# Dealing one weight matrix anew over the DMA engines of a decode kernel

## The chip, the cores and the metric

One core of a Trainium2 chip. The time is the device time of one execution in microseconds (us), lower is better. Engines are named as in the profile: PE (TensorE), DVE (VectorE), ACT (ScalarE), POOL (GpSimd), SP (SyncE, which here only issues transfers). The core has sixteen DMA engines.

## The reference

A decode step for four tokens: the input goes through a layer norm, and the sum of three things is returned: the input, an attention block over a cache (A), and a small gated MLP (B).

```python
x = A_x                                     # 4 x 1 x 640
xn = _layernorm(x, axis=-1)
# A: 32 heads of 128, a cache of 4096 positions for each of the 4 tokens
q = (xn @ wq) ...                           # wq 640 x 4096
scores = jnp.einsum('bhqd,bhkd->bhqk', q, k_cache) * Dh ** (-0.5)
p = _softmax(scores, axis=-1)
o = jnp.einsum('bhqk,bhkd->bhqd', p, v_cache)
A = o... @ wo                               # wo 4096 x 640
# B: F = 1728, Fh = 864
z = _gelu(jnp.einsum('bsd,df->bsf', xn, w_in))      # w_in 640 x 1728
z1 = z[..., :Fh]
z2 = _layernorm(z[..., Fh:], axis=-1)
g = jnp.einsum('ts,bsf->btf', w_sp, z2) + b_sp[None, :, None]
B = jnp.einsum('bsf,fd->bsd', z1 * g, w_out)        # w_out 864 x 640
return x + A + B
```

All data is bf16. The two caches are 128 MiB each; the other weights together are about 14 MB.

## The kernel before

**What streams.** K and V come in units: eight heads of one token, 4 MiB, laid on 128 partitions of 64 KiB. There are 16 units of K and 16 of V. The tile `kv` has five slots of 32 KiB per partition, and a unit takes two halves of slots; the dictionary `place` says which. SP issues all these loads from one queue, in the order of `seq`: K0 to K3, then V0, K4, V1, K5 and so on (`load_unit`, line 187). The fourth unit of K of each group of heads and the last unit of V are loaded in two parts (`cuts`). Each load waits until the engines have done with what lay in its slots. A unit is 64 KiB on each partition and eight partitions on each DMA engine.

**A unit of K** (`emit_K`): DVE transposes it in eight instructions (line 419, some 2.3 us each) into the two halves of `kT_t`, and PE multiplies (line 430). After four units come the softmax and the spreading of its weights (`softmax`, `z_fill`). **A unit of V** (`emit_V`): 64 matmuls (line 501), then two DVE instructions. **The end:** the last three parts of A_wo (`load_wo`, line 195), the projections (`o_mul`, line 544), one sum, and the output.

**The start.** SP issues wq (line 126) and w_in (line 129) first. The MLP's second matrix, w_out, lies in the tile `w_words`, which the K transposes use afterwards (`kT_t` is its first part). It is kept as 26 chunks of 640 on 128 partitions; row (partition, chunk) holds one of the 864 rows of w_out, and the places that hold none must be zero. So DVE fills the 8,320 words of each partition with zeros (line 131), and then six pieces are loaded. The table `PC` describes a piece: first and last partition and their step, first chunk, chunks n, the factor i by which its rows are dealt, and the run of consecutive rows:

```python
PC = {"w": (0, 28, 2, 0, 9, 7, 9), "a": (32, 52, 1, 0, 10, 5, 10), "n": (68, 92, 2, 0, 8, 6, 8),
      "l": (92, 95, 1, 0, 26, 2, 13), "b": (1, 12, 2, 0, 26, 3, 26), "s": (60, 68, 1, 0, 26, 2, 26)}
```

`load_piece` (line 136) gives a piece to a queue; the source's outermost dimension is i. Before, SP loads "a" and "b"; GpSimd, with a queue of its own, loads "w", "s", "n" and "l" in that order. Between them SP loads four `marks` (line 144): a few bytes of w_out to 6, 10, 12 and 14 partitions of a scratch tile that nothing reads. A transfer ends by counting up a semaphore; SP's and ACT's transfers use eight of these in turn, and one that takes a semaphore again first waits for the transfer that had it before.

**The MLP.** `xnT` is the normalised input, turned. z is computed by matmuls of 32 columns of PE each (line 328; five chunks c, six matmuls each, into three column groups q and two PSUM tiles `zr_ps`). ACT applies gelu in 16 instructions (`gelu`, lines 339 and 342), which put the columns in their places in `zT`. Then come the statistics (lines 365 to 380), three POOL instructions (381 to 383), a DVE transpose (384), and 52 matmuls with w_out (line 397). Only after the first sixteen of these may the first K unit be transposed into `w_words`; and only when half of it is transposed (four instructions) is the slot free that the third K load needs.

Of the kernel before, what the change touches and what calls it, by code (L numbers as in the profile page):

```python
# [8 lines left out]
ACT = mybir.ActivationFunctionType  # L9
# [3 lines left out]
BF16 = mybir.dt.bfloat16  # L13
# [3 lines left out]
def kernel(  # L17
# [19 lines left out]
    nc = tc.nc  # L37
    P = 128
    B, Sq, D = A_x.shape
    _, H, Sk, Dh = A_k_cache.shape  # L40
    assert Sq == 1 and B == 4 and Dh == P and D % P == 0
    DC = D // P
# [14 lines left out]
    FC = 26  # L57
# [3 lines left out]
    PC = {"w": (0, 28, 2, 0, 9, 7, 9), "a": (32, 52, 1, 0, 10, 5, 10), "n": (68, 92, 2, 0, 8, 6, 8),  # L61
          "l": (92, 95, 1, 0, 26, 2, 13), "b": (1, 12, 2, 0, 26, 3, 26), "s": (60, 68, 1, 0, 26, 2, 26)}
    f_of, f_end = {}, 0
# [4 lines left out]
    NOUT = A_wo.shape[1]  # L68
# [3 lines left out]
    eps = 1e-5  # L72
# [58 lines left out]
    nc.vector.memset(w_words[:, 0:FC * NOUT // 2], 0.0)  # L131
# [7 lines left out]
    load_piece(nc.sync, "a")  # L139
    load_piece(nc.sync, "b")  # L140
    marks = const.tile([14, 288], BF16)
    m0 = 0
    for k, m in ((6, 96), (10, 80), (12, 64), (14, 48)):
        nc.sync.dma_start(out=marks[0:k, m0:m0 + m], in_=B_w_out[0:k, 0:m])
        m0 += m
    sw = load_piece(nc.gpsimd, "w")
    for t in ("s", "n", "l"):
        with tc.issue_after(sw.ins):
            sw = load_piece(nc.gpsimd, t)
# [55 lines left out]
    nc.gpsimd.memset(ones_f[:], 1.0)  # L205
    eps_t = const.tile([P, 1], F32)
    nc.gpsimd.memset(eps_t[:], eps)
# [39 lines left out]
    nc.gpsimd.memset(SelN[:].rearrange("p e x -> p (e x)"), 0.0)  # L247
# [57 lines left out]
    for a in range(2):  # L305
# [13 lines left out]
    z_parts = [(0, 0, w_z[:, :, :, f_of["w"][0]:f_of["w"][1]]), (0, 1, w_z[:, :, :, f_of["a"][0]:f_of["a"][1]]),  # L319
               (0, 2, w_z[:, :, :, f_of["n"][0]:f_of["l"][1]]), (1, 0, w_z[:, :, :, f_of["b"][0]:f_of["b"][1]])]  # L320
    s_src = w_z[:, :, :, f_of["s"][0]:f_of["s"][1]].rearrange("p d a (r i c) -> p d i a r c", i=2, c=PC["s"][4])
    z_parts += [(1, 1 + i, s_src[:, :, i]) for i in range(2)]
    for c in range(DC):
        for bk, q, src in z_parts:
            w = 1
            for m in src.shape[3:]:
                w *= m
            nc.tensor.matmul(zr_ps[bk][32 * q:32 * q + 32, :, 0:w], lhsT=xnT[:, c, :], rhs=src[:, c],  # L328
                             start=(c == 0), stop=(c == DC - 1))
# [4 lines left out]
    def gelu(q, bk, f0, c0, n, x, order=None):  # L334

        z = zr_ps[bk][32 * q:32 * q + 32, :, f0:f0 + len(range(*x)) * n]
        dst = zT[32 * q:32 * q + 32, :, c0:c0 + n, x[0]:x[1]:x[2]]
        if order is None:
            nc.scalar.activation(out=dst, in_=z.rearrange("p a (x c) -> p a c x", c=n), func=ACT.Gelu_apprx_tanh)
        else:  # L340
            for a in range(2):
                nc.scalar.activation(out=dst[:, a].rearrange("p c (i r) -> p c i r", i=order),  # L342
                                     in_=z[:, a].rearrange("p (r i c) -> p c i r", i=order, c=n), func=ACT.Gelu_apprx_tanh)

    gelu(0, 0, 0, 0, 9, (0, 28, 2), 7)
    gelu(1, 0, 0, 0, 10, (0, 20, 1), 5)
    gelu(2, 0, 0, 0, 8, (4, 28, 2), 6)
    f_l = f_of["l"][0] - f_of["n"][0]
    for i in range(2):
        for j in range(3):  # L350
            x = 28 + (3 * i + j) // 2
            gelu(2, 0, f_l + 26 * j + 13 * i, 13 * ((3 * i + j) % 2), 13, (x, x + 1, 1))
    gelu(0, 1, 0, 0, 26, (1, 12, 2), 3)
    gelu(1, 1, 0, 0, 26, (28, 32, 1))
    gelu(2, 1, 0, 0, 26, (0, 4, 1))

    one_bf = const.tile([1, P], BF16)
    nc.gpsimd.memset(one_bf[:], 1.0)
# [284 lines left out]
```

## Time and profile before

| | us |
|---|---|
| median of 3 runs (663.44 to 663.63) | 663.45 |
| the profiled execution's own time | 663.37 |
| its span, first to last instruction | 661.6 |
| DVE busy | 380.1 |
| PE busy | 293.2 |
| wq first packet | 1.7 |
| zero fill of w_out's tile on DVE | 2.53 to 9.52 |
| z matmuls | 25.57 to 28.29 |
| gelu instructions | 29.49 to 32.56 |
| first K transpose | 46.89 |
| third K load issued | 56.03 |
| last transfer of A_wo landed | 658.27 |

On the page, "DMA" is the mean busy share of the sixteen DMA engines in each fortieth of the span, in tenths; q1 is the queue of SP, q0 that of GpSimd, q10 that of ACT, q8 and q14 carry the engines' instructions.

The trace has the start, length, size and queue of each of the 7,112 packets, but not the DMA engine. In a busy stretch a packet starts some 4 ns before or 2 to 3 ns after the end of the one before it on its engine, so the packets can be joined into sixteen streams. From 10 us to the end of A_wo all sixteen then carry the same 368 packets of wq, w_in, K, V and A_wo, each in the same order; they differ in these things alone:

| streams | pieces of w_out on each | bytes of w_out | end of K0, us | instruction fetches on the way | end of the last A_wo packet, us |
|---|---|---|---|---|---|
| 3 | a, b, w | 140,800 | 44.37, 44.54, 44.73 | none | 657.01, 657.17, 657.30 |
| 2 | a, w | 74,240 | 42.22, 42.24 | one and three of 8 KB | 655.67, 657.83 |
| 2 | w | 23,040 | 40.14, 40.54 | two of 16 KB each | 655.99, 656.33 |
| 2 | s | 133,120 | 44.45, 45.14 | one of 8 KB each | 657.78, 657.81 |
| 6 | n | 20,480 | 39.91 to 40.72 | two of 16 KB; the last stream three | 655.69, 655.77, 655.77, 655.88, 656.50, 657.46 |
| 1 | l | 99,840 | 44.03 | none | 656.67 |

(Where two streams are within some 10 ns of each other they can be taken for one another; this happens among the six "n" streams and near 20 us.) The 16 KB fetches come 49.8, 76.2, 113.1, 151.4, 189.9, 229.4, 258.6, 287.4 us after the start, on eight different streams, and then go round the same eight again in the same order; the 17th (634.3) falls to the first and the 18th comes at 656.4.

### The profile page before, as it was taken

The page shows a single profiled execution, that of the slowest core. Times are in us where ns is not written, and L with a number is a line of the kernel's source. Part 1 is how long each engine was busy: PE and PEld are TensorE (multiplying, and loading weights), DVE is VectorE, ACT ScalarE, POOL GpSimd, SP SyncE. Part 2 cuts the span into 40 slices and gives each one's busy share as a digit, 9 for nine tenths or more (in the row PEclk, how much of TensorE's full clock was granted, in tenths as well). Part 3 has the DMA queues.
Part 4 walks back from the last instruction along what each step waited for, and adds up shares of the span by engine and source line. Part 5 has one row for each costly group of instructions (what it writes and reads, how often), then busy time and mean ns, then how long its engine had stood idle before and what let it go on. Part 6 is the DMA issues. An engine that isn't in the chain of part 4 may idle for free.

```text
span 661.6 us, 5493 instructions
## 1 busy us (share of the span) xinstructions
PE 293.2 (44%) x2273; PEld 109.6 (17%) x2273; DVE 380.1 (57%) x307; ACT 75.2 (11%) x152; POOL 73.1 (11%) x140
## 2 busy tenths in 40 slices
PE   0436565447063355334426075642607255541236
PEld 0222111112021121111102022210202112120113
DVE  6239989756191758718346196764619175971112
ACT  0310000340100000330200000070100000042200
POOL 5341000030200000130300000030110000002300
PEclk9858878768567686776858578665857758766678
DMA  9999999999999999999999999999999999999997
GB/s 371 463 434 409 429 440 441 440 432 417 432 433 444 437 408 433 440 441 436 429 432 416 445 422 437 442 429 428 440 433 428 437 432 413 456 428 421 431 420 289
DMA packets 7098, 282.60 MB, mean 427 GB/s; under 512 B 1116, under 2 KB 1376, under 8 KB 1632
## 3 DMA queue, kind: packets, MB, share of 16 engines
q1 hardware_dynamic: 6758, 281.60, 98.8%
q0 software_dynamic: 288, 0.65, 0.3%
q8 instruction: 18, 0.29, 0.2%
q14 instruction: 6, 0.05, 0.0%
q10 hardware_dynamic: 28, 0.01, 0.0%
HBM read 282.25 MB, written 0.01 MB: 427 GB/s over the span
## 4 chain that ended last, share of the span: by engine, by line
DMA 71%; DVE 12%; issue 11%; PE 3%; POOL 1%; ACT 1%; SPq 0%; DVEq 0%; POOLq 0%; ACTq 0%
DMA kv<-in_A_k_cache_dram 59%; DVE w_words L419 10%; DMA kv<-in_A_v_cache_dram 5%; DMA kv<-in_B_w_in_dram 4%; DMA kv<-in_A_wo_dram 4%; PE O L501 1%; PE proj L397 1%; POOL kv L381 0%; PE misc L328 0%; DVE w_words L481 0%; DVE w_words L463 0%; PE S L430 0%; POOL z_b L383 0%; ACT kv L342 0%; POOL kv L366 0%
## 5 line engine op out<-in xcount | busy, mean ns | idle before, releaser
L419 DVE STREAM_TRANSPOSE w_words<-kv 128x2048 f32<-128x2048 f32 x128 | 282.9, 2276 | 118.1 <-DMA kv<-in_A_k_cache_dram 115.9
L430 PE MATMUL S<-w_words,QZ 128*32 128x512 bf16 x1024 | 190.6, 506 | 247.2 <-DVE w_words L419 247.1
L430 PEld LDWEIGHTS <-QZ 128*32 128x32 bf16 x1024 | 60.4, 112 | 374.4 <-issue 312.1
L501 PE MATMUL O<-kv,w_words 128*32 128x512 bf16 x1024 | 75.4, 459 | 56.3 <-DMA kv<-in_A_v_cache_dram 45.7
L467 ACT ACTIVATE w_words<-w_words,MkE 32x128 bf16<-32x128 bf16 x120 | 60.9, 508 | 118.0 <-PE O L501 104.9
L510 DVE TENSOR_TENSOR om<-O,Mk 128x512 f32<-128x512 f32 x15 | 10.4, 692 | 95.1 <-PE O L501 95.1
L465 POOL TENSOR_SCALAR w_words<-w_words,MkE 32x128 bf16<-32x128 bf16 x60 | 43.0, 716 | 139.5 <-PE O L501 127.1
L501 PEld LDWEIGHTS <-w_words 128*32 128x32 bf16 x1024 | 34.0, 113 | 97.9 <-issue 69.0
L475 ACT ACTIVATE w_words<-S,negmax 128x1024 bf16<-128x1024 f32 x4 | 4.5, 1114 | 396.3 <-DVE negmax L447 396.3
L463 DVE TENSOR_SCALAR w_words<-w_words,MkE 32x128 bf16<-32x128 bf16 x76 | 24.8, 326 | 2.3
L405 POOL COPY QZ<-qT 32x32 bf16<-32x32 bf16 x16 | 5.1, 316 | 170.4 <-PE S L430 169.8
L511 DVE TENSOR_REDUCE R<-om 128x128 f32<-128x512 f32 x15 | 15.3, 1020 | 0.5
L486 POOL TENSOR_SCALAR rs<-MkB,rowsum 128x4 f32<-128x4 f32 x4 | 1.2, 299 | 112.4 <-ACT w_words L475 112.4
L481 DVE STREAM_TRANSPOSE w_words<-w_words 128x1024 bf16<-128x1024 bf16 (+1 forms) x8 | 9.6, 1241 | 5.6 <-ACT w_words L475 5.6
L534 POOL MEMSET oT<- 128x66 bf16 x4 | 0.5, 156 | 97.9 <-PE proj L544 97.9
L397 PE MATMUL proj<-w_words,z_b 128*8 128x320 bf16 (+1 forms) x52 | 5.6, 394 | 8.8 <-DVE z_b L384 8.8
L131 DVE MEMSET w_words<- 128x8320 f32 x1 | 7.0, 6992 | 2.5 <-issue 2.5
L513 DVE TENSOR_SCALAR R<-O,Mk 128x128 f32<-128x128 f32 x1 | 0.3, 350 | 14.1 <-PE O L501 14.1
L437 DVE TENSOR_REDUCE m<-S 128x1 f32<-128x1024 f32 x4 | 4.9, 1224 | 5.6 <-PE S L430 5.6
L523 PE MATMUL misc<-R,SelX 128*128 128x512 f32 x8 | 4.5, 644 | 7.2 <-DVE R L511 5.5
L299 PE MATMUL q<-kv,xnT 128*32 128x512 bf16 x40 | 4.2, 603 | 6.2 <-DVE xnT L228 6.2
L488 PE MATMUL misc<-rs,SelE 128*128 128x4 f32 x8 | 2.2, 339 | 10.4 <-POOL rs L486 10.4
(100 smaller groups left out, 89.3 us busy)
## 6 DMA issues: line engine op xcount, KB each, us to landing
kv<-in_A_k_cache_dram SPq DMA_DIRECT2D x8, 4096.0 KB
kv<-in_A_v_cache_dram SPq DMA_DIRECT2D x1, 6144.0 KB
kv<-in_A_wq_dram SPq DMA_DIRECT2D x1, 5120.0 KB
kv<-in_A_wo_dram SPq DMA_DIRECT2D x3, 1280.0 KB
kv<-in_B_w_in_dram SPq DMA_DIRECT2D x1, 2160.0 KB, 24.4
kv<-in_A_v_cache_dram SPq DMA_DIRECT2D x1, 2048.0 KB
kv<-in_A_wo_dram SPq DMA_DIRECT2D x1, 640.0 KB
kv<-in_A_wo_dram SPq DMA_DIRECT2D x1, 320.0 KB, 23.9
```

Source lines behind the costliest of these rows:

```text
L131: nc.vector.memset(w_words[:, 0:FC * NOUT // 2], 0.0)
L397: nc.tensor.matmul(proj[r0:r0 + nb, 0:NO2], lhsT=uT[:, u0:u0 + nb], rhs=w_out[:, fc, hf * NO2:(hf + 1) * NO2], start=(fc == 1 and hf == 0) ...
L405: nc.gpsimd.tensor_copy(out=QZ[r0:r0 + 32, :, :, :, 8 + 8 * hp], in_=qT[32 * g:32 * g + 32, NE * hp:NE * hp + NE].rearrange("p e a b -> p ...
L419: nc.vector.transpose(kT.rearrange("p (t r) -> p t r", r=32), kw)
L430: nc.tensor.matmul(S_ps[32 * q:32 * q + 32, i], lhsT=QZ[:, b, 2 * kh + w, e, w0:w0 + 32], rhs=kb[:, i, :, e, :, w], start=(b == 0 and k < ...
L463: nc.vector.tensor_scalar(out=dst, in0=src, scalar1=mk, scalar2=None, op0=ALU.mult)
L465: nc.gpsimd.tensor_scalar(out=dst, in0=src, scalar1=mk, scalar2=None, op0=ALU.mult)
L467: nc.scalar.activation(out=dst, in_=src, func=ACT.Copy, scale=mk)
L481: nc.vector.transpose(pT_t[:, j0:j1, :], blocks)
L501: nc.tensor.matmul(O_ps[32 * q:32 * q + 32, :, :], lhsT=Zb[b % 2][:, w].rearrange("p h c -> p (h c)"), rhs=vv[:, w * 4 * Dh:(w + 1) * 4 * ...
L510: nc.vector.tensor_tensor(out=om4[:], in0=O_ps[:], in1=Mk4[:, :, None].to_broadcast((P, 4, Dh)), op=ALU.mult)
L511: nc.vector.tensor_reduce(out=R, in_=om4[:].rearrange("p c d -> p d c"), axis=AX.X, op=ALU.add)
```

## The change

Seven pieces instead of six. "w" gets 15 chunks instead of 9 and goes to SP's queue; "a" is 10 partitions of 8 chunks instead of 20 of 10; "s" 23 chunks instead of 26; "n" is split into "n" (8 partitions of 17 chunks, i = 4) and "m" (4 of 5, i = 2). The bytes of each of the sixteen shares:

| piece | queue before, shares x bytes | queue after, shares x bytes |
|---|---|---|
| w | GpSimd, 7 x 23,040 | SP, 7 x 38,400 |
| a | SP, 5 x 51,200 | SP, 5 x 20,480 |
| b | SP, 3 x 66,560 | SP, 3 x 66,560 |
| s | GpSimd, 2 x 133,120 | GpSimd, 2 x 117,760 |
| n | GpSimd, 6 x 20,480 | GpSimd, 4 x 43,520 |
| m | | GpSimd, 2 x 12,800 |
| l | GpSimd, 1 x 99,840 | GpSimd, 1 x 99,840 |

GpSimd's queue first gets a small transfer to the scratch tile `walk` (14 partitions, i = 7, as the old "w" had), which stands where "w" stood in the turn of that queue. The four marks become two steps of SP's queue (4 and 8 partitions). The zero fill is split at chunk 15 between DVE (4,800 words) and GpSimd (3,520). Four small constant fills go from GpSimd to DVE. z is computed in the order in which the pieces need it: 14 matmuls for each of the five chunks instead of 6, and 8 gelu instructions instead of 16.

```diff
@@ -58,8 +58,9 @@
-    PC = {"w": (0, 28, 2, 0, 9, 7, 9), "a": (32, 52, 1, 0, 10, 5, 10), "n": (68, 92, 2, 0, 8, 6, 8),
-          "l": (92, 95, 1, 0, 26, 2, 13), "b": (1, 12, 2, 0, 26, 3, 26), "s": (60, 68, 1, 0, 26, 2, 26)}
+    PC = {"w": (0, 28, 2, 0, 15, 7, 15), "a": (32, 52, 2, 0, 8, 5, 8), "b": (1, 12, 2, 0, 26, 3, 26),
+          "s": (60, 68, 1, 0, 23, 2, 23), "n": (68, 84, 2, 0, 17, 4, 17), "m": (84, 92, 2, 0, 5, 2, 5),
+          "l": (92, 95, 1, 0, 26, 2, 13)}
     f_of, f_end = {}, 0
     for t, (p0, p1, st, _, n, _, _) in PC.items():
         f_of[t] = (f_end, f_end + len(range(p0, p1, st)) * n)
@@ -128,7 +129,11 @@
     w_in = at_slot(2, n_in).rearrange("p (c f) -> p c f", c=DC)
     nc.sync.dma_start(out=w_in, in_=B_w_in.rearrange("(p c) f -> p c f", c=DC))
-    nc.vector.memset(w_words[:, 0:FC * NOUT // 2], 0.0)
+    walk = const.tile([14, 256], BF16)
+    sw = nc.gpsimd.dma_start(out=walk[:, 0:128], in_=B_w_out[0:14, 0:128].rearrange("(r i) n -> i r n", i=7))
+    MS = 15 * NOUT // 2
+    nc.vector.memset(w_words[:, 0:MS], 0.0)
+    nc.gpsimd.memset(w_words[:, MS:FC * NOUT // 2], 0.0)
     w_out = w_words[:, 0:FC * NOUT // 2].bitcast(BF16).rearrange("p (c n) -> p c n", c=FC)
     def load_piece(eng, t):
@@ -136,15 +141,13 @@
         return eng.dma_start(out=w_out[p0:p1:st, c0:c0 + n].rearrange("p c n -> p (c n)"),
                              in_=B_w_out[f_of[t][0]:f_of[t][1], :].rearrange("(r i c) n -> i r (c n)", i=k, c=run))
-    load_piece(nc.sync, "a")
-    load_piece(nc.sync, "b")
-    marks = const.tile([14, 288], BF16)
-    m0 = 0
-    for k, m in ((6, 96), (10, 80), (12, 64), (14, 48)):
-        nc.sync.dma_start(out=marks[0:k, m0:m0 + m], in_=B_w_out[0:k, 0:m])
+    for t in ("w", "a", "b"):
+        load_piece(nc.sync, t)
+    m0 = 128
+    for k, m in ((4, 72), (8, 56)):
+        nc.sync.dma_start(out=walk[0:k, m0:m0 + m], in_=B_w_out[0:k, 0:m])
         m0 += m
-    sw = load_piece(nc.gpsimd, "w")
-    for t in ("s", "n", "l"):
+    for t in ("s", "n", "m", "l"):
         with tc.issue_after(sw.ins):
             sw = load_piece(nc.gpsimd, t)
@@ -202,9 +205,9 @@
     ident_f = const.tile([P, P], F32)
     make_identity(nc, ident_f[:])
     ones_f = const.tile([P, P], F32)
-    nc.gpsimd.memset(ones_f[:], 1.0)
+    nc.vector.memset(ones_f[:], 1.0)
     eps_t = const.tile([P, 1], F32)
-    nc.gpsimd.memset(eps_t[:], eps)
+    nc.vector.memset(eps_t[:], eps)
     lnb = ln_t[:XR, D:7 * D].bitcast(F32)
     xf, xc, sq = lnb[:, 0:D], lnb[:, D:2 * D], lnb[:, 2 * D:3 * D]
@@ -244,7 +247,7 @@
     i2 = I32[:].rearrange("p (pr c) -> p c pr", c=C2)
     nc.gpsimd.tensor_tensor(out=SelP[:], in0=i2[:, 0], in1=i2[:, 1], op=ALU.add)
     SelN = const.tile([P, NE, HP * B], F32)
-    nc.gpsimd.memset(SelN[:].rearrange("p e x -> p (e x)"), 0.0)
+    nc.vector.memset(SelN[:].rearrange("p e x -> p (e x)"), 0.0)
     for q in range(4):
         nc.gpsimd.tensor_scalar(out=SelN[32 * q:32 * q + 32, q % 2], in0=SelP[32 * q:32 * q + 32, :], scalar1=-scale,
                                 scalar2=None, op0=ALU.mult)
@@ -316,46 +319,45 @@
     zr_ps = [misc_ps([P, 2, 256], F32) for _ in range(2)]
-    z_parts = [(0, 0, w_z[:, :, :, f_of["w"][0]:f_of["w"][1]]), (0, 1, w_z[:, :, :, f_of["a"][0]:f_of["a"][1]]),
-               (0, 2, w_z[:, :, :, f_of["n"][0]:f_of["l"][1]]), (1, 0, w_z[:, :, :, f_of["b"][0]:f_of["b"][1]])]
-    s_src = w_z[:, :, :, f_of["s"][0]:f_of["s"][1]].rearrange("p d a (r i c) -> p d i a r c", i=2, c=PC["s"][4])
-    z_parts += [(1, 1 + i, s_src[:, :, i]) for i in range(2)]
+    z_in = {(0, 0): ('w',), (0, 1): ('a', 's'), (0, 2): ('n', 'm', 'l'), (1, 0): ('b',), (1, 2): ('s',)}
+    z_at_col, z_parts = {}, []
+    for (bk, q), names in z_in.items():
+        col, parts = 0, []
+        for t in names:
+            p0, p1, st, _, n, k, run = PC[t]
+            x0, x1 = max(p0, 32 * q), min(p1, 32 * q + 32)
+            m = len(range(x0, x1, st)) * n
+            assert col + m <= 256
+            src = w_z[:, :, :, f_of[t][0]:f_of[t][1]].rearrange("p d a (r i c) -> p d a r i c", i=k, c=run)
+            dst = zr_ps[bk][32 * q:32 * q + 32, :, col:col + m]
+            if x1 - x0 < p1 - p0:
+                parts.append((dst, src[:, :, :, :, (x0 - p0) * k // (p1 - p0)]))
+            elif run < n:
+                d_i = dst.rearrange("p a (i f) -> p i a f", i=k)
+                parts += [(d_i[:, i], src[:, :, :, :, i]) for i in range(k)]
+            else:
+                d_r = dst.rearrange("p a (i r c) -> p r a i c", i=k, c=n)
+                parts += [(d_r[:, r], src[:, :, :, r]) for r in range(m // (k * n))]
+            z_at_col[bk, q, t] = (col, m, n, PC[t][3], x0 - 32 * q, x1 - 32 * q, st)
+            col += m
+        z_parts.append(parts)
     for c in range(DC):
-        for bk, q, src in z_parts:
-            w = 1
-            for m in src.shape[3:]:
-                w *= m
-            nc.tensor.matmul(zr_ps[bk][32 * q:32 * q + 32, :, 0:w], lhsT=xnT[:, c, :], rhs=src[:, c],
-                             start=(c == 0), stop=(c == DC - 1))
+        for parts in z_parts:
+            for j, (dst, src) in enumerate(parts):
+                nc.tensor.matmul(dst, lhsT=xnT[:, c, :], rhs=src[:, c], start=(c == 0 and j == 0),
+                                 stop=(c == DC - 1 and j == len(parts) - 1))
     z_f = at_slot(2, 2 * 3 * NB, z_at).bitcast(F32).rearrange("p (a n) -> p a n", a=3)
     z_b = [ppool.tile([P, NB], BF16, tag="p", name=f"z_b{i}") for i in range(2)]
     zT = z_f[:, 0:2, :].rearrange("p a (i j) -> p a i j", j=32)
     nc.gpsimd.memset(z_f[:, 0:2, :], 0.0)
-    def gelu(q, bk, f0, c0, n, x, order=None):
-
-        z = zr_ps[bk][32 * q:32 * q + 32, :, f0:f0 + len(range(*x)) * n]
-        dst = zT[32 * q:32 * q + 32, :, c0:c0 + n, x[0]:x[1]:x[2]]
-        if order is None:
-            nc.scalar.activation(out=dst, in_=z.rearrange("p a (x c) -> p a c x", c=n), func=ACT.Gelu_apprx_tanh)
-        else:
-            for a in range(2):
-                nc.scalar.activation(out=dst[:, a].rearrange("p c (i r) -> p c i r", i=order),
-                                     in_=z[:, a].rearrange("p (r i c) -> p c i r", i=order, c=n), func=ACT.Gelu_apprx_tanh)
-
-    gelu(0, 0, 0, 0, 9, (0, 28, 2), 7)
-    gelu(1, 0, 0, 0, 10, (0, 20, 1), 5)
-    gelu(2, 0, 0, 0, 8, (4, 28, 2), 6)
-    f_l = f_of["l"][0] - f_of["n"][0]
-    for i in range(2):
-        for j in range(3):
-            x = 28 + (3 * i + j) // 2
-            gelu(2, 0, f_l + 26 * j + 13 * i, 13 * ((3 * i + j) % 2), 13, (x, x + 1, 1))
-    gelu(0, 1, 0, 0, 26, (1, 12, 2), 3)
-    gelu(1, 1, 0, 0, 26, (28, 32, 1))
-    gelu(2, 1, 0, 0, 26, (0, 4, 1))
+    for (bk, q, t), (col, m, n, c0, x0, x1, st) in z_at_col.items():
+        rows = slice(32 * q, 32 * q + 32)
+        nc.scalar.activation(out=zT[rows, :, c0:c0 + n, x0:x1:st],
+                             in_=zr_ps[bk][rows, :, col:col + m].rearrange("p a (x c) -> p a c x", c=n),
+                             func=ACT.Gelu_apprx_tanh)
     one_bf = const.tile([1, P], BF16)
-    nc.gpsimd.memset(one_bf[:], 1.0)
+    nc.vector.memset(one_bf[:], 1.0)
     sb_ps = misc_ps([P, 2], F32)
     nc.tensor.matmul(sb_ps[:], lhsT=one_bf[:], rhs=sb_bf[:], start=True, stop=True)
     sb_f = const.tile([P, 2], F32)
```

## The prediction

> **What bounds the kernel now.** I read the slices and queues of the page first, then the chain that ended last, the timeline of the first 60 us, the waits of SP's queue, and the DMA packets behind them.
>
> ```profile
> span 661.6 us, 5493 instructions
> DMA  9999999999999999999999999999999999999997
> q1 hardware_dynamic: 6758, 281.60, 98.8%
> q8 instruction: 18, 0.29, 0.2%
> DMA 71%; DVE 12%; issue 11%; PE 3%; POOL 1%; ACT 1%; SPq 0%; DVEq 0%; POOLq 0%; ACTq 0%
> ```
>
> The DMA digit is 9 in 39 of 40 slices, and SP's queue q1 alone takes 98.8% of the engines' time. So what counts is bytes per DMA engine, and any moment in which an engine has nothing queued.
>
> ```profile
> 633.06 23.63 DMA kv<-in_A_wo_dram
> 656.68 0.04 issue
> 656.73 0.44 PE proj L544 x4
> ```
>
> The tail (chain of waits, 640 us on) hangs on the last pieces of A_wo: PE starts its last matmuls as they land. The slowest engine's last A_wo packet ends at 657.83 and lands at 658.27; the rest to 661.6 is fixed. If that engine ends earlier or later, the kernel does.
>
> Each packet record starts within some 15 ns of the end of one before it, so I joined them into sixteen streams (front table). Between 30 and 658 us only one stream ever stands empty, for 133 ns. The last packets end between 655.67 and 657.83, mean 656.67. Perfect levelling would thus win 1.16 us and no more, and 0.2% of 663.45 us, about what a measurement of this kernel can tell from no change, is 1.3 us.
>
> ```profile
> 2.53 6.99 DVE L131 MEMSET w_words<- 128x8320 f32 x1 [2.53 <-issue]
> ...
> 9.55 1.74 SPq L136 DMA_DIRECT2D w_words<-in_B_w_out_dram  x2
> 9.84 2.63 POOL L136 DMA_DIRECT2D w_words<-in_B_w_out_dram  x4 [5.62 <-DVE w_words L131]
> ...
> 11.34 5.58 SPq L144 DMA_DIRECT2D marks<-in_B_w_out_dram  x4
> ...
> 16.96 57.36 SPq L187 DMA_DIRECT2D kv<-in_A_k_cache_dram  x5
> ...
> 25.57 2.72 PE L328 MATMUL misc<-kv,xnT 128*32 128x252 bf16 x30 [3.80 <-DMA kv<-in_B_w_in_dram]
> ```
>
> ```profile
> SPq L187 <- DVE w_words L419: 47.1, 3, 29.9
> SPq L187 <- DMA kv<-in_B_w_in_dram: 8.2, 1, 8.2
> SPq L144 <- DMA kv<-in_A_wq_dram: 4.0, 1, 4.0
> ```
>
> These are the start: fill, w_out pieces, K loads; and SP's waits. A mark waits 4.0 us for wq (its semaphore is used again), and the first K load (k0, 16.96) stands behind it. The third (k2) waits for DVE's transposes of k0 and is issued at 56.03.
>
> **The new deal.** In the trace a piece takes as many streams as its factor i (7, 5, 3, 2, 6; "l" one), SP's pieces nested on the same first ones, GpSimd's one after the other. By packet rows (12,800 B 0.479 us, 33,280 B 1.232, 11,520 B 0.432, 10,240 B 0.385; 37 ns per 1,000 B for new sizes): the three a+b streams go from 1.92+2.46+0.86 to 1.43+0.77+2.46 us, -0.58; the two a-only streams -0.58; the two w-only streams 0.86 to 1.43, +0.56; the two "s" streams 4x1.232 to 4x1.091, -0.56; of six "n" streams four get 1.62 for 0.77, +0.85, and two ("m") 0.49, -0.28; "l" 0. Put on the table's ends this gives 656.43 to 656.72; 655.09 and 657.25; 656.55 and 656.89; 657.22 and 657.25; "l" 656.67; four "n" up to 657.35.
>
> **Instruction fetches.** Eighteen 16 KB packets of q8 go round eight streams (six "n", two w-only). Each costs its stream about 1.5 us (20.98 against 19.43 us for the same V load at 634). The 17th makes three on one stream (657.46); the 18th, whose turn is the second stream's, comes at 656.4, too late to matter. The z stage goes from 30 to 14x5 = 70 matmuls, 80 more PE instructions with their weight loads, and a fetch comes every 256 or so: the 18th moves 40 matmuls forward, into the last V unit (near 649), and adds 1.5 to the second stream. Which "n" streams are these? Turns 3 and 4 are the w-only pair; ascending order then starts at the last two of the six, the "m" streams. I take that: 657.46-0.28 = 657.18 and 655.69-0.28+1.5 = 656.91. If they were among the four, the first would end at 657.46+0.85 = 658.31. The Trainium skill (Runtime: NRT & Kernel Launch, "Instruction fetch mechanics") calls a 16 KiB crossing mostly hidden. By it the 18th would cost nothing; the trace shows it hidden for PE, not for the DMA engine.
>
> So with every queue full, the slowest goes from 657.83 to 657.35: -0.48 us.
>
> **The fill.** DVE's 6.99 us for 8,320 words becomes 4.0 for 4,800, done at 6.6. GpSimd's 3,520 words at 0.89 ns (1,664 in 1.48 us, L333) take 3.1, inside its 5.62 us idle; the four small memsets (0.1 to 0.2 each) go to DVE, which waits for x until 10.7. "s" can be issued at 6.6 to 7.6 instead of 10.5. That is no gain by itself: SP's pieces queue behind w_in, which ends at 20 to 21 on their streams; if that cover were gone, the fill's 3 us would show. But GpSimd's queue alternates with q1 packet by packet. Its first load, issued at 9.84, was not in the rings at 13.55 and was at 13.88 (3.7 to 4.0 us), so "s" arrives at 10.3 to 11.6. On its two streams wq packets end at 10.3/10.5, 11.8/12.0 and 13.3/13.5: two "s" packets of 1.09 now fall ahead of the end of wq, which goes from 14.85/15.06 to 17.0/17.2 and lands at 17.6 (16.2 before). If the walk's empty turns hold "s" back one packet it is one, and wq lands at 16.5; three need "s" in the rings before 10.3.
>
> **The queue behind it.** Counting semaphores in order, the second step (m=56) uses wq's again, as the third mark did. Two marks less save 0.4 us, but k0 stands behind the step: 17.6+0.4 = 18.0, against 16.96. How soon must it come? At 56.03 k2 was issued, and at 59.24 to 59.26 four streams needed it: three found it, one was empty until 59.40. Issue to ring is 3.2 to 3.4 us under load; k0 is there at 21.2 to 21.4. The "m" streams run dry at about 20.3 and 20.5 (20.57, 20.80 less 0.28), the "n" and w-only ones at 21.4 or later. So two streams stand idle 0.7 to 1.1 us; lower bound 0, if an unloaded ring is quicker: wq's first packets came 1.0 to 1.6 us after issue. I take 0.8 and 1.0, nearest to the k2 row. Ends: 657.98 and 657.91; the slowest is 657.98, +0.15. The Trainium skill (DMA: Bandwidth & Descriptors, "Latency and other measured facts") gives about 0.6 us to HWDGE's first byte; by it no stream runs dry and the sum stays -0.48. The k2 row speaks against it.
>
> **z and gelu.** Within a column group starts follow at columns/1.2 ns without gap (312 columns 260 ns). Per chunk the fullest group goes from 608 to 732 columns: 5x732/1.2 = 3.05, with 0.2 of drain 3.24 for 2.72, +0.52 (strictly in order it would be 4.66, +1.94). w_in lands 0.56 earlier, as its slowest streams carry "s". Eight gelu instructions less at 0.066 us (26 columns take 97 ns, 208 take 340): -0.53. Sum -0.57 (in order +0.85); K transposes and k2 move with it, to 55.5, so k2 is no longer short. If it were late by 0.85, the second "m" stream would stop 1.2 us instead of 1.0: 658.1.
>
> **Sum.** 663.37 (span 661.6 and 1.8 around it) +0.15 = 663.52; the median of the runs is 0.08 higher: 663.6. The levelling is real and is given back by two dry streams.
>
> **Rivals.** (1) k0 in time: one "s" packet ahead of wq's end, or a ring quicker than k2's. For it: wq's own 1.0 us; against: the 133 ns hole. 663.45-0.48 = 662.97. (2) Slower: the z matmuls set k2. If 70 cost 91 ns each, the mean spacing of the 30, z takes 6.35 us, k2 goes out at 56.03+3.63-0.56-0.53 = 58.6 and is there at 61.9; the second "m" stream is dry at 58.97, so it ends at 656.91+2.9 = 659.8, +2.0: 665.4. It decides from z over some 5.7 us. Against it: no gap inside a group, and at 657.5 matmuls start every 33 ns. (3) Three "s" packets ahead: wq lands at 18.7, k0 goes at 19.1, the first "m" stream loses 1.9: 659.1, 664.7. (4) The step of GpSimd's queue does not move the next piece to the eighth stream: "s" falls on two streams that carry a and b, 4.4 us more there, some 666.7. The old "w" had the same shape and did move it.
>
> **Numbers.** Forecast 0.57 (with the fetches on other streams, 663.9, inside it), rivals 0.27, 0.08, 0.05, 0.03. Range 662.8 to 664.9: the first rival, the forecast with 0 to 1.9 us of dry streams; left out are (2), (4) and tails. Faster by over 0.2% asks for more than perfect levelling: 0.03. Slower: (2), (4), half of (3): 0.14. Within: 0.83.
>
> **What would show it.** Right: DVE's fill near 4 us, 70 matmuls at L328 of about 3.2 us, k0 issued near 18, a hole of 0.5 to 1.1 us on two streams at 20 to 21.5, k2 before 56, last A_wo packets between 656.4 and 658.1. Wrong: k0 at or before 17 with no hole (rival 1); z over 5 us and k2 past 57.5 (rival 2); three fetches on a stream that carries 43,520 B.

## The result

The changed kernel is slower: it takes 664.97 us (median of 14 runs, 664.65 to 665.43), and the kernel before takes 663.49 beside it (663.35 to 663.81, 14 runs). The ratio is 1.0023, with a 95% interval of 1.0014 to 1.0031. The forecast was 663.6 with a range of 662.8 to 664.9: the first K load (k0) was held back in the way that was forecast, but four packets stood ahead of what it waits for and not two, and it left at 20.13 us instead of 18.0.

**The profile after.** The profiled execution took 664.99 us. First the page: span, queues and the shares of the chain that ended last.

```profile
span 663.1 us, 5569 instructions
DMA  9999999999999999999999999999999999999996
q1 hardware_dynamic: 6709, 281.71, 98.6%
q8 instruction: 18, 0.29, 0.2%
DMA 74%; DVE 12%; issue 11%; PE 2%; ACT 0%; SPq 0%; DVEq 0%; ACTq 0%
```

Little here gives the loss away: the DMA digit is 9 as before, q1's share of the engines' time fell by 0.2 points in a span 1.5 us longer, and only the loads' share of the last chain rose, from 71% to 74%. The tail, from the chain of waits, shows only that all of it comes from the loads:

```profile
633.37 24.96 DMA kv<-in_A_wo_dram
658.33 0.04 issue
658.38 0.44 PE proj L546 x4
```

PE's `proj` matmuls start 1.65 us later than before (656.73). What follows them takes 4.7 us (4.9 before). The start, from the timeline (start, length, engine and line):

```profile
1.79 4.06 DVE L135 MEMSET w_words<- 128x4800 f32 x1 [1.79 <-issue]
2.21 3.05 POOL L136 MEMSET w_words<- 128x3520 f32 x1
5.95 2.56 SPq L141 DMA_DIRECT2D w_words<-in_B_w_out_dram  x3
6.16 2.29 POOL L141 DMA_DIRECT2D w_words<-in_B_w_out_dram  x4 [0.24 <-DVE eps_t L210]
8.55 11.53 SPq L148 DMA_DIRECT2D walk<-in_B_w_out_dram  x2
20.13 6.86 SPq L190 DMA_DIRECT2D kv<-in_A_k_cache_dram  x2
25.34 1.91 PE L347 MATMUL misc<-kv,xnT 128*32 128x210 bf16 x70 [1.72 <-DMA kv<-in_B_w_in_dram]
```

```profile
SPq L148 <- DMA kv<-in_A_wq_dram: 10.8, 1, 10.8
```

The second group of lines is from SP's list of waits: the second walking step waits 10.8 us for wq (the mark of before waited 4.0), and k0 leaves at 20.13 instead of 16.96. z took 1.91 us for 70 matmuls, less than the 30 took before (2.72). The granted clock differs: in the windows view, before first, it is the third number from the right.

```profile
25.50:28.30 2.80, 2.72 (x30) 2.17 (x30) 0.00 (x0) 0.10 (x1) 0.64 (x2) 0.52 0.99 427
```

```profile
25.30:27.30 2.00, 1.91 (x70) 1.80 (x70) 0.96 (x1) 0.06 (x1) 0.87 (x3) 1.00 0.32 139
```

Now the packets, joined into sixteen streams as in the prediction. The first 's' packet starts at 10.53 on one stream and 11.71 on the other, so by then it stood in the rings, ready for the DMA engine. On the first, three of them (10.53, 13.12, 15.72) run ahead of the end of wq, whose last data packet there ends at 18.32; then a fourth runs for 1.09 us before wq's completion word (the 4-byte packet that counts up the semaphore, at 19.41), and the step goes at 19.80.

Then k0. Six streams stand empty for 6.0 us in all, the longest for 2.33. But that is less than half of the loss. Ten streams start their first k0 packet between 21.4 and 22.6, and all ten packets end between 24.95 and 25.43; the one that began at 21.43 took 3.91 us instead of 2.42. K0's packets are 9.0 us longer than 128 times 2.42, where those of the kernel before are 0.8 longer. A stretched packet counts as busy, so the DMA digit doesn't see it. The rate does: here is the stretch 20 to 24 us from the windows view, before first, then after (the last three columns: granted clock, DMA share, GB/s).

```profile
20.00:24.00 4.00, 1.77 (x20) 0.58 (x13) 1.52 (x2) 0.59 (x1) 0.91 (x6) 1.00 1.26 531
```

```profile
20.00:24.00 4.00, 3.62 (x40) 1.43 (x33) 0.33 (x1) 0.00 (x0) 2.68 (x14) 1.00 1.13 415
```

From 60 to 640 us both move 432 GB/s. The ends of the last A_wo packets:

```
                      mean     latest   streams with three instruction fetches
before                656.67   657.83   657.46
after                 657.54   659.53   659.53, 659.42
k0 first (below)      656.64   657.42   657.42, 656.99
```

The mean went up by 0.87. The two streams that carry three instruction fetches were meant to be the ones with a head start, and they had to wait for k0 like the others; the third fetch then stands on top.

### The profile page after: what moved, and what is told of

Same layout as the page of the kernel before. It is cut to its first block, busy times and chain, and to the rows that moved or that the text cites. A ratio compares the mean times of both kernels' runs of the same rounds, so it can differ in the third digit from the quotient of the medians.

```text
span 663.1 us, 5569 instructions
## 1 busy us (share of the span) xinstructions
PE 284.8 (43%) x2313; PEld 108.3 (16%) x2313; DVE 377.4 (57%) x311; ACT 74.7 (11%) x144; POOL 76.4 (12%) x138
## 4 chain that ended last, share of the span: by engine, by line
DMA 74%; DVE 12%; issue 11%; PE 2%; ACT 0%; SPq 0%; DVEq 0%; ACTq 0%
DMA kv<-in_A_k_cache_dram 63%; DVE w_words L421 10%; DMA kv<-in_A_v_cache_dram 5%; DMA kv<-in_A_wo_dram 4%; DMA kv<-in_A_wq_dram 3%; PE O L503 1%; DVE w_words L483 0%; PE S L432 0%; DVE w_words L465 0%; DVE m L439 0%; ACT w_words L477 0%; PE proj L546 0%; DVE o_q L602 0%; DVEq L421 0%; PE misc L443 0%
## 5 line engine op out<-in xcount | busy, mean ns | idle before, releaser
L432 PE MATMUL S<-w_words,QZ 128*32 128x512 bf16 x1024 | 186.0, 496 | 255.3 <-DVE w_words L421 255.3
L503 PE MATMUL O<-kv,w_words 128*32 128x512 bf16 x1024 | 72.7, 447 | 58.1 <-DMA kv<-in_A_v_cache_dram 47.6
L546 PE MATMUL proj<-kv,oT 128*8 128x320 bf16 x54 | 5.6, 350 | 1.3 <-DMA kv<-in_A_wo_dram 1.3
```

Source lines behind the costliest of these rows:

```text
L432: nc.tensor.matmul(S_ps[32 * q:32 * q + 32, i], lhsT=QZ[:, b, 2 * kh + w, e, w0:w0 + 32], rhs=kb[:, i, :, e, :, w], start=(b == 0 and k < ...
L503: nc.tensor.matmul(O_ps[32 * q:32 * q + 32, :, :], lhsT=Zb[b % 2][:, w].rearrange("p h c -> p (h c)"), rhs=vv[:, w * 4 * Dh:(w + 1) * 4 * ...
L546: nc.tensor.matmul(dst[0:nb, 0:n1 - n0], lhsT=state[("oT", g)][:, c0:c0 + nb], rhs=wo_t[g][:, c, n0:n1], start=start, stop=stop)
```

## The experiments

The theory was that k0's delay is the whole loss and that the deal itself is a gain. The rival was that the deal is wrong, with its third fetch on two streams.

### k0 first

```diff
-    for k, m in ((4, 72), (8, 56)):          # ahead of k0 on SP's queue
-        nc.sync.dma_start(out=walk[0:k, ...], ...)
     load_unit(seq[0])                        # k0
+    for k, m in ((4, 72), (8, 56)):
+        nc.sync.dma_start(out=walk[0:k, ...], ...)
```

> The changed kernel, with one difference: on SyncE's queue the first K load (k0) goes out ahead of the two walking steps, so that it no longer stands behind the step that waits for wq's semaphore. Theory (k0 late): in the changed kernel k0 was issued at 20.13 us; the streams' mean end rose by 0.87 us (656.67 to 657.54), and empty time (6.0 us over six streams) plus first k0 packets that took up to 3.9 us instead of 2.42 (some 7.6 us over all) are 13.6 us over sixteen streams, 0.85 each. With k0 issued near 9 us both vanish: k0's packets take 19.3 to 19.5 us on every stream, the mean end comes back to about 656.7, the stream that ended at 659.53 to about 656.9, the other with three fetches from 659.42 to about 657.9; time 663.5 (662.9 to 663.9). Rival (the new deal itself, with a third instruction fetch on two streams, costs the time): the slowest stream stays at 659 or later, 664.6 or more.

Measured: 662.76 us (662.69 to 662.93, 11 runs) beside 663.41 before, ratio 0.9990 (0.9982 to 0.9999), 0.14 below the expected range. From the timeline and the chain of waits:

```profile
8.54 0.46 SPq L186 DMA_DIRECT2D kv<-in_A_k_cache_dram  x1
19.67 0.62 SPq L199 DMA_DIRECT2D walk<-in_B_w_out_dram  x2
```

```profile
632.62 23.63 DMA kv<-in_A_wo_dram
656.25 0.04 issue
656.29 0.44 PE proj L546 x4
```

The steps still wait for wq until 19.67 (three 's' packets ahead of its end, as in the changed kernel), but nothing that matters stands behind them. No stream is empty, every k0 packet takes 2.42 us but for the one that shares its time with a fetch, and the rate in the same stretch is back at 484 GB/s with the very DMA share of the changed kernel, 1.13:

```profile
20.00:24.00 4.00, 3.49 (x40) 1.46 (x33) 0.46 (x1) 0.00 (x0) 2.39 (x14) 1.00 1.13 484
```

So moving two transfers is worth 2.2 us: k0's delay cost all that was lost and the gain of the deal besides. The rival is out. The two streams with three fetches are here plainly the 'm' streams (6,400 B pieces), as the prediction took them to be.

### The whole fill on DVE

```diff
-    nc.vector.memset(w_words[:, 0:MS], 0.0)
-    nc.gpsimd.memset(w_words[:, MS:FC * NOUT // 2], 0.0)
+    nc.vector.memset(w_words[:, 0:FC * NOUT // 2], 0.0)
```

> The changed kernel with the whole zero fill on VectorE as before, GpSimd's half left out; the deal, the steps and z stay. Theory (the shared fill lets the 's' pieces into wq, wq lands late and k0 with it): the fill ends near 8.8 us, 's' is issued near 9 and has at most one packet ahead of wq's end, wq lands between 16.2 and 17.4, k0 goes out between 16.6 and 17.8 instead of 20.13, light streams lose 0 to 0.5 us, slowest stream 657.6 to 658.2, time 663.3 to 663.9. Rival (k0's time is set by something else, or does not matter): k0 near 20, 664.6 to 665.3.

Measured: 662.82 us (662.70 to 662.93 in nine of 11 runs, and 663.91 and 664.46), ratio 0.9994 (0.9985 to 1.0003); the median is 0.5 below the expected range, and the runs of 663.91 and 664.46 have no profile. From the timeline:

```profile
12.17 4.31 SPq L146 DMA_DIRECT2D walk<-in_B_w_out_dram  x2
16.53 57.00 SPq L188 DMA_DIRECT2D kv<-in_A_k_cache_dram  x5
24.67 3.32 PE L345 MATMUL misc<-kv,xnT 128*32 128x210 bf16 x70 [2.40 <-DMA kv<-in_B_w_in_dram]
```

The fill ends 3.7 us later, and the kernel is 2.1 us faster: 's' first moves at 14.67, when wq's data is nearly all there (its last packet ends at 15.62), and k0 leaves at 16.53. The latest stream ends at 657.39. In the changed kernel, then, k0's delay goes when the fill is no longer shared; the step behind wq passes it on.

### The shared fill in the kernel before

```diff
-    nc.vector.memset(w_words[:, 0:FC * NOUT // 2], 0.0)
+    MS = 15 * NOUT // 2
+    nc.vector.memset(w_words[:, 0:MS], 0.0)
+    nc.gpsimd.memset(w_words[:, MS:FC * NOUT // 2], 0.0)
```

> The kernel before with one part of the change alone: the zero fill shared by VectorE (4,800 words) and GpSimd (3,520). Theory: GpSimd's pieces are issued some 3 us earlier, two 's' packets of 1.23 us and the completion's turn behind a third fall ahead of wq's landing, which goes from 16.2 to 18.5 to 19.5; the fourth mark and k0 behind it go out at 18.9 to 19.9 instead of 16.96, the light streams' first k0 packets end about 1.1 us later or more, the slowest (the w-only stream with three fetches, 657.46, and the heavy ones at 657.8) ends at 658.2 to 659; time 663.9 to 664.6, slower with nothing gained. Rival (an earlier fill is harmless or a gain): 663.45 or less, k0 at or before 17.

Measured: 663.39 us (663.21 to 663.54, 11 runs), ratio 0.9998 (0.9989 to 1.0007): a miss.

```profile
7.66 9.60 SPq L146 DMA_DIRECT2D marks<-in_B_w_out_dram  x4
17.30 57.15 SPq L189 DMA_DIRECT2D kv<-in_A_k_cache_dram  x5
```

k0 left at 17.30, only 0.34 later. There 'w' stands ahead of 's' in GpSimd's queue, and its small packets (11,520 B, 0.43 us) go over seven streams: the first 's' packet moved at 14.96, after nearly all of wq, whose last data packet ended at 16.08. So the shared fill does no harm by itself. What differs in the changed kernel is GpSimd's order, in which 's', four packets of 1.09 us on each of two streams, is the first piece. That this order lets 's' in early was not tested apart. A quicker fill brought nothing in either order: here 663.39 beside 663.41, and 662.76 (k0 first) beside 662.82 (fill on DVE).

### Forty more matmuls in the kernel before

```diff
+    for i in range(40):
+        nc.tensor.matmul(zr_ps[0][0:32, 0, 0:32], lhsT=xnT[:, 0, :], rhs=ident_bf[:, 0:32], start=True, stop=True)
     for c in range(DC):
         for bk, q, src in z_parts:
```

> The kernel before with 40 matmuls of 32 columns added ahead of z, where TensorE waits for w_in, into a tile that z overwrites: 80 more TensorE instructions and nothing else. If the instruction fetches go by the count of TensorE's instructions and each holds one DMA stream: the 18th fetch comes forward from 656.4 to about 649, the stream that it falls on ends near 657.8 instead of 656.33, the sum of the sixteen ends rises by 1.4 to 1.6 us, and the time stays at 663.4 to 663.6. Otherwise: the fetch stays where it was, or the stream's end does not move.

Measured: 663.62 us (one run; 663.4 to 663.6 expected). The matmuls lie in PE's idle time, at 21.38 in the timeline:

```profile
21.38 1.16 PE L324 MATMUL misc<-ident_bf,xnT 128*32 128x32 bf16 x40
25.43 2.72 PE L330 MATMUL misc<-kv,xnT 128*32 128x252 bf16 x30 [2.89 <-DMA kv<-in_B_w_in_dram]
```

The 18th fetch came at 652.9 instead of 656.4 (649 expected), within 1 us of where e.g. the k0-first kernel has it (652.2). The stream that took it ends at 657.23 (657.8 expected); those with the same pieces and two fetches end at 655.7 to 656.3 in this trace. So it holds that stream by 0.9 to 1.5 us, while the latest end belongs to another (658.09, a stream with w, a and b). The fetches go by PE's count, and the change's 40 matmuls bring the 18th in time to matter.

### The marks behind k0 in the kernel before

```diff
-    for k, m in ((6, 96), (10, 80), (12, 64), (14, 48)):   # ahead of k0
+    ...                                                    # the same loop behind load_unit(seq[0])
```

> The kernel before with its four marks moved behind k0 on SyncE's queue, the same edit as in the first experiment. Theory: k0, issued at 16.96 in the kernel before, was in time there (no empty stream, every k0 packet 2.42 us), so issuing it near 11.5 brings nothing: 663.3 to 663.5, latest stream 657.7 to 657.9. Rival (an earlier k0 is a gain by itself, and the first experiment's 662.76 owes nothing to the new deal): 662.7 to 662.9.

Measured: 663.34 us (663.27 to 663.53, 11 runs), ratio 0.9998 (0.9989 to 1.0007). k0 leaves at 11.31 and nothing comes of it; the latest stream ends at 657.71. From the timeline:

```profile
11.31 0.45 SPq L183 DMA_DIRECT2D kv<-in_A_k_cache_dram  x1
```

An early k0 is no gain by itself. That leaves the new deal, with its order of z, for what the k0-first kernel gains over the kernel before (0.65 us). The latest stream end shows 0.4 of this (657.83 to 657.42); the rest is not explained.

### How late may k0 be

Three kernels, and one of them a second time, vary k0's issue in the changed kernel. The fill cut at 20 columns:

```diff
-    MS = 15 * NOUT // 2
+    MS = 20 * NOUT // 2
```

> The changed kernel with the fill cut at 20 of 26 columns instead of 15: VectorE's part 5.4 us, done at 7.2, 's' issued near 7.4 instead of 6.2, in the rings at 11.4 to 11.9 instead of 10.5; one packet fewer of 's' ahead of wq's end, wq's landing near 18, k0 at 18.2 to 18.9 instead of 20.13. Theory (a first k0 packet ends 4.8 to 5.3 us after k0's issue, or when the stream comes to it, 22.85 to 23.24 on the 'm' streams, whichever is later): 23.0 to 24.2, the 'm' streams lose 0 to 1.1 us, slowest stream 657.4 to 658.5, time 662.8 to 663.8. Rival (a k0 that stands behind wq costs its 2.2 us however early wq lands): 664.6 to 665.2.

Measured: median 663.76 us, but spread from 662.75 to 664.96 (11 runs), where the kernel before stays within 0.4. The profiled execution took 662.89. Hence a second profile of the same kernel:

> The kernel with the fill cut at 20 columns once more, for a second profile: its runs lay between 662.75 and 664.96, where those of the kernel before lie within 0.4, and the profiled one was at the lower end (662.89, k0 at 17.93, first k0 packets of the 'm' streams ending at 23.2 and 23.3). Theory (how many 's' packets get ahead of wq's end differs from run to run, and k0 and the end with it): a run over 663.8 has k0 at 18.9 or later and first packets of 2.9 us or more; a run near 662.9 looks like the first profile. Rival: the time differs with k0 at the same place.

This one took 664.68. SP's queue in the two timelines, the first and the second:

```profile
10.22 7.67 SPq L148 DMA_DIRECT2D walk<-in_B_w_out_dram  x2
17.93 7.52 SPq L190 DMA_DIRECT2D kv<-in_A_k_cache_dram  x2
```

```profile
10.23 8.49 SPq L148 DMA_DIRECT2D walk<-in_B_w_out_dram  x2
18.78 7.29 SPq L190 DMA_DIRECT2D kv<-in_A_k_cache_dram  x2
```

In the second, 's' was in one stream's ring at 11.78 instead of 13.09 or later, wq's last data packet ended at 16.98 instead of 16.13, and k0 left 0.85 us later. (The expectation asked for 18.9 and first packets of 2.9 us; it was 18.78 and 2.89.) One ring filled a packet sooner makes 1.8 us at the end: that is the spread.

A third step behind the other two was to hold k0 until w_in:

```diff
     for k, m in ((4, 72), (8, 56)):
         ...
+    late = const.tile([16, 32], BF16)
+    nc.sync.dma_start(out=late[:], in_=B_w_out[0:16, 0:32])
```

> The changed kernel with a third step of 16 rows behind the other two (the dealing place comes back to where it was), whose semaphore is w_in's: k0 stands behind w_in's landing as well and goes out near 25.7 us instead of 20.13. Theory: the light streams' first k0 packets end at 30.5 to 31.0 instead of 24.95 to 25.43, every stream is empty meanwhile, the end moves by the same 5.6 us: 670.5 (669.5 to 671.5). Rival (the tail is set by the deal and by the fetches, k0's delay is taken up on the way, since 40 later loads wait on the engines and not on it): under 667.

Measured: 665.47 us (665.29 to 665.70, 7 runs). The step's semaphore was not w_in's, and k0 left at 20.44, only 0.31 later than in the changed kernel; the expectation's 670.5 was for another k0. So the copy was taken out of w_in's tile instead:

```diff
+    nc.sync.dma_start(out=late[:], in_=w_in[0:16, 0, 0:32])
```

> The changed kernel with a third step behind the other two that copies 16 rows of 32 columns out of w_in's tile, so that it, and k0 behind it, wait until w_in has landed, near 25.3 us: k0 at 25.6 to 25.9 instead of 20.13. Theory (nothing takes up a late k0 on the way to the end): first k0 packets end 4.8 to 5.3 us after the issue, at 30.4 to 31.2, all sixteen streams are empty before, and the end moves as k0 does, 5.6 us: 670.5 (669.5 to 671.5). Rival (a later k0 is partly taken up by slack in the loads behind it): 666 to 669.

Measured: 670.05 us (670.00 to 670.13, 4 runs), ratio 1.0098 (1.0083 to 1.0113), as the theory had it. Timeline, and the windows of 17 to 26 us:

```profile
24.85 0.63 SPq L151 DMA_DIRECT2D late<-kv  x1
25.53 1.95 SPq L192 DMA_DIRECT2D kv<-in_A_k_cache_dram  x2
```

```profile
17.00:20.00 3.00, 0.33 (x4) 0.23 (x8) 0.52 (x2) 0.00 (x0) 2.63 (x9) 1.00 0.99 420
20.00:23.00 3.00, 3.00 (x32) 1.25 (x28) 0.00 (x0) 0.00 (x0) 2.63 (x14) 1.00 0.59 245
23.00:26.00 3.00, 2.28 (x61) 1.50 (x54) 1.19 (x2) 0.59 (x1) 0.00 (x0) 1.00 0.15 62
```

Only here does the DMA share show the hole. All together, by k0's issue, from the profiled executions:

```
                   k0     first k0 packets end    K0's packets beyond   latest A_wo    time
                          (of streams free early)   128 x 2.42 us        packet ends
k0 first            8.54   22.85 on (not late)      0.5                  657.42       662.90
fill on DVE        16.53   not late                 0.5                  657.39       662.93
20 columns         17.93   23.17, 23.30             1.2                  657.40       662.89
20 columns again   18.78   24.00 to 25.09           4.8                  659.17       664.68
changed kernel     20.13   24.95 to 25.43           9.0                  659.53       664.99
third step         20.44   25.39 to 25.84          10.8                  660.00       665.70
behind w_in        25.53   29.76 to 30.83          10.7                  664.41       670.09
```

In these executions a later k0 costs nothing up to 17.9; from there the end follows the first packets. From the changed kernel to the last row k0 moves by 5.40 us and the profiled time by 5.10. The mean end moves by 3.9 (657.54 to 661.48), as the heavy streams, with work left until 24 to 25 us, lose less than the light ones. Next to nothing on the way of 640 us takes up the delay, though nearly all the later loads wait for engines and not for k0.

### Two tries at more level streams

Both start from the k0-first kernel and move columns between the pieces.

```diff
-  "w": 15, "a": 8,  "b": 26, "s": 23, "n": 17, "m": 5      # columns n, changed kernel
+  "w": 15, "a": 11, "b": 21, "s": 25, "n": 17, "m": 1      # first try
+  "w": 16, "a": 7,  "b": 22, "s": 26, "n": 18, "m": 2      # second try
```

> The first experiment's kernel (k0 ahead of the walking steps) with the pieces dealt once more by its stream ends (latest 657.42, one of the two streams with three instruction fetches and 'm'; 656.99 the other; the three with w, a and b 656.57 to 657.25; lightest 654.80, with w and a): 'm' 5 columns to 1, 's' 23 to 25, 'a' 8 to 11, 'b' 26 to 21, the sum kept. At 0.048 us for a column's 1,280 B: the two 'm' streams -0.39 (657.03, 656.60), the b streams 2x(3-5) columns, -0.19 (657.06 at most), the a-only ones +0.29, the 's' streams +0.38 (656.8 at most). Theory (with every queue full the slowest stream sets the time): 657.42 to about 657.05, 662.76 to 662.4 (662.2 to 662.6). Rival (the level of the streams no longer matters, something else bounds the end): 662.76.

> The first experiment's kernel with a second try at level streams, from the ends of both: w 16 columns, a 7, b 22, s 26, n 18, m 2 (15, 8, 26, 23, 17, 5 in the changed kernel; the sum kept). The try before left one stream with w and a at 657.29, which the 8 KB fetches of another queue load. At 0.048 us for 1,280 B, from the ends of that try: w and a 657.00, w with a and b 656.81, s 656.96, n 657.05, m 656.95 at most. Theory (the slowest stream sets the time): 657.05 instead of the first experiment's 657.42, 662.4 (662.2 to 662.7). Rival (what is left is not in the deal): 662.76 to 662.9.

Measured: 662.91 (662.79 to 663.16, ratio 0.9992, 0.9983 to 1.0001) and 662.73 (662.61 to 662.93, ratio 0.9988, 0.9980 to 0.9997). The first is a miss. Its 'm' streams did end at 656.85 and 656.58, but a stream with w and a came out at 657.29: its like with the same pieces ended at 654.99. That stream was already the 657.00 of the k0-first kernel, against 654.80; the six 8 KB fetches of queue q14, some 0.31 us each, make 1.9 of the 2.2 between them if they all fall on it, which was not shown apart (in the table of the kernel before they are joined to four streams). The second try ends at 657.16 in the trace (an 's' stream, 0.2 beyond its expectation), 0.26 earlier than the k0-first kernel; between the medians, 662.73 and 662.76, no difference can be told, and 662.73 lies just above the expected range (662.2 to 662.7) and below the rival's. Both beat the kernel before by about what the plain k0-first kernel does, and what the deal had left to give is in the noise.

## Why the prediction was wrong

**Right: what bounds, and the worth of the deal.** With every queue full the prediction had the slowest stream at 657.35 and 662.97 us. The k0-first kernel, which is just that case, ends at 657.42 and takes 662.76. The third fetch on the first two streams of the round and the 'm' streams as its bearers came as worked out; the 18th fetch was brought forward, but to 652 to 654 us and not to 649. That the two ends agree to 0.1 us is in part luck: the slowest was to be an 'n' stream, and it is the first 'm' stream (657.42, forecast 657.18).

**The step that failed: what goes ahead of wq's landing.** The forecast was this very mechanism, 's' ahead of wq's end, the step that waits, k0 behind it, empty streams. But it let two 's' packets go ahead of wq's data and none after that, so wq was to land at 17.6 and k0 to leave at 18.0. The step that waits for wq went at 19.80 and k0 at 20.13. Two more 's' packets of 1.09 us make up these 2.1 us.

1. *A third packet ahead of wq's data.* DVE's fill began at 1.79 instead of 2.53, 's' went into GpSimd's queue at 6.16 instead of 6.6 to 7.6, and the packet that starts at 10.53 lies inside the forecast's 10.3 to 11.6. For three packets the forecast asked for 's' before 10.3, where a wq packet ends on one of its two streams. On the other that happens at 10.5 by the same list, and 10.53 came just in time there. So wq's data ended at 18.32 instead of 17.2. The rival with three packets and k0 at 19.1 (664.7, given 0.05) was nearly what happened.
2. *A fourth ahead of wq's completion word.* This term the prediction put at nothing: it counted 's' packets against wq's data alone, and the word takes one more turn in the alternation. In four traces what waits for wq goes 1.47 to 1.50 us after wq's last data packet, where an 's' packet of 1.09 stands behind that (19.80 after 18.32, 19.67 after 18.20, 18.47 after 16.98, 17.63 after 16.13). In five traces where none stands there it goes after 0.34 to 0.58 (before, fill on DVE, and the three other kernels made from the one before). The second profile of the fill at 20 columns has this term almost alone. Two packets got ahead, and wq's data ended at 16.98, as the forecast had it (17.0 to 17.2), yet k0 left at 18.78 and that run took 664.68.

**Wrong in kind, but not too small: what a late k0 costs.** The prediction took 3.2 to 3.4 us from issue to ring, from k2, and full speed from there, so a first packet would end 5.6 to 5.8 after the issue. By the table above most end 4.2 to 5.4 after it, at the latest 6.3 (20 columns again). In the last row of the table, where all streams were empty, the first k0 packets start 1.20 us after the issue, but thirteen of the sixteen take 3.0 to 3.4 us instead of 2.42. In the changed kernel they start 1.3 us after it and take up to 3.9. So much of the loss sits inside the first packet, where neither an empty stream nor the DMA digit shows it. The two 'm' streams were given 0.8 and 1.0; against the k0-first kernel they lost 2.0 (657.42 to 659.42) and 2.5 (656.99 to 659.53). With k0 at 20.13 and the prediction's own price they would have lost 2.9 and 3.1, ending at 660.1 (about 665.7 us). So this term did not cause the miss; it hid part of it. And in the first profile of the fill at 20 columns, with k0 at 17.93 as forecast, the latest end is 657.40 and not 657.98.

**Too narrow: who loses.** Dry streams were looked for only where a stream ran empty before k0's arrival, at the two 'm' streams. The stretched packets hit ten, and the mean end of all sixteen is 0.9 later than in the k0-first kernel (6.0 us empty and 8.5 us of longer packets, over sixteen: 0.91). The slowest two are the 'm' streams all the same.

The Trainium skill (DMA: Bandwidth & Descriptors, "Latency and other measured facts") gives about 0.6 us to HWDGE's first byte, which the prediction set aside for the k2 row. The 1.20 us here lie between the two, and the first byte was not the price: the whole first packet was. The same page of the Trainium skill ("Queues, rings and completion order") has an engine take turns between queues by whole packets; the traces agree, with 29,440 B of 's' (1.09 us) between any two of the last packets of wq (1.51 us) on the 's' streams and before the completion word.

**Wrong, without harm: z.** 3.24 us were predicted, 1.91 measured, and k2 left at 54.95 (55.5 predicted). The prediction took its rate, 1.2 columns per ns, from a stretch whose granted clock was 0.52, and kept it; in the changed kernel that stretch reads 1.00, and the 3,660 columns of the fullest group in 1.91 us are 1.9 per ns. The rival in which z sets k2 has nothing for it. k2's earlier issue brought nothing, since its queue was not short.

**What the chances missed.** 0.83 lay on "within 0.2%". The miss is near a case on the list, but the range was cut too short: its upper end adds the third rival's 1.9 us of dry streams to the levelled kernel, and so allows for three packets ahead of wq's data and for nothing ahead of its completion word.

## What to carry to other kernels

Before a queue is made to start earlier, list what stands in line behind it on the *other* queues: here four packets on one DMA engine held back one weight's completion, a helper transfer of under 1 KB waited for that, and the 4 MiB load behind the helper waited for both. Put the load that keeps all engines fed ahead of any transfer that may wait for a semaphore; it cost two moved transfers and turned +1.5 us into -0.65. And when a busy share says 9 everywhere, compare the bytes moved in the same stretch: engines that hold a packet they can't finish count as busy.

## What the hardware showed that was not expected

- A load that reaches empty engines stretches its first packets: 3.0 to 3.4 us for 64 KiB with all streams empty (thirteen of sixteen), up to 3.9 where some still worked, 2.42 when the load had been queued in time. What the engine waits for inside the packet was not shown.
- A queue's completion word takes its turn like a packet: some 1.5 us from wq's last data packet to the instruction that waits, where an 's' packet of 1.09 us stood in the other queue, and 0.34 to 0.58 where none did.
- The time of z goes with the granted clock: 70 matmuls took 1.90 to 2.11 us in the six profiles that read 1.00 there, and 2.68 and 3.07 in the two of the fill at 20 columns, which read 0.64 and 0.56. The 3.32 of the fill on DVE can't be placed: its trace holds no clock record before 47.4 us, so the 1.00 that the view gives there is no reading. PE had stood idle for 0.7 to 1.7 us before the quick ones and for 2.3 to 3.1 before the others; whether this sets the clock was not tested.
- A kernel can be on the edge: with k0 leaving at 17.9 to 18.8 us, the same program's runs spread over 2.2 us. With k0 at 16.53 in the profile, two of 11 runs lay 1.0 to 1.8 us above the rest (they have no profile, so their cause is open); with k0 at 8.54 all lie within 0.3, and with k0 at 20.13 within 0.8.
